# Longformer attention fused with a squared-ReLU expert layer: the order of work in batch 0, and where batch 2's waiting time is filled

## The chip, the cores and the metric

The kernel runs on one NeuronCore of a Trainium2 chip. The core has five engines with a queue of instructions each: TensorE (PE in the profile, its weight loads PEld), VectorE (DVE), ScalarE (ACT), GpSimd (POOL) and SyncE (SP). Sixteen DMA engines move data between the device memory (HBM) and the core's on-chip SBUF; transfers issued by POOL go through the queue q0 (software_dynamic), those of SP and ACT through q1 and q10 (hardware_dynamic). Matrix products land in PSUM, eight banks of 128 x 512 float32.

The metric is the device time of one execution in microseconds (us), as the median of several runs. A profiled execution is one more run with every instruction recorded; its span runs from the first to the last instruction of the program, and its own time is a little more than its span.

## What is computed

```python
B, H, S, D = 8, 8, 576, 64           # q, k, v: (B, H, S, D); 8 global tokens
scores = q @ k.T / sqrt(D)
mask = abs(i - j) <= 32  or  i is global  or  j is global
attn = softmax(where(mask, scores, -1e9))
x = (attn @ v).transpose(0, 2, 1, 3).reshape(4608, 512)
h = maximum(x @ w_in, 0)             # w_in: (512, 2048)
out = (h * h) @ w_out                # w_out: (2048, 512)
```

All inputs and the output are float32; the kernel computes in float16 with float32 sums.

## The kernel before

**Tiling.** The attention goes by pairs of heads: 8 batches of 4 pairs, numbered i = 4 b + hp. The 576 queries of a pair are padded to 608 columns (four groups of 144 tokens and the 8 global tokens again after each) and handled in two halves of 304. For a half, `sc_mm` makes the scores of the windows (S^T, keys on the partitions) in a PSUM tile `at`; `sc_exp` (ACT) takes their exponential; `sc_mask` (DVE) multiplies it with the 0/1 mask. In batch 0, where `added` says so, the mask is instead added to the scores by a product of the identity with the tile `far`. `pv_mm` multiplies with v and with ones into another `at` tile, `pv_rec` (ACT: logarithm, exponential) inverts the sums, `pv_mul` (DVE) writes the normalized result into `xT` (batch 0: first half into `xA`). `pv_sum` (DVE) collects the global queries' rows, and `scatter` (POOL, eight small copies at positions that are read from the input by `load_columns`) writes them over their tokens' columns.

**The expert layer** goes by chunks of 256 or 512 tokens, `CHUNKS`. For chunk 0, `mm1_half(u, half, tiles)` multiplies two of 16 blocks of w_in's columns with 256 tokens; `tiles` are the four groups of 128 input features, one for each pair of heads, so that the sum over pairs can stop after some of them and go on later. `mm2` adds up the output in four parts. From chunk 1 on, `mm1` (8 products) is followed by `mm2_fast`, which makes the second product from seven block products (Strassen's scheme, 14 pieces of 16 products): `g_sum` (DVE) adds blocks of the squared activations, and `weight_sum(p)` (DVE, once each for p = 1, 3, 4, 6, 7) adds blocks of w_out into the buffer `early`.

**Order.** Every engine runs its instructions in the order in which the program lists them. Batch 0's is written out by hand (lines 900 to 1013): the second query half of pair 0 and of pair 1 is mixed in among the first halves of pairs 2 and 3. From batch 1 on, expert work stands in a list `fills` of `(n, function, arguments)`, where n is the number of batches whose attention must be done. `fill(c)` adds c to a credit and takes entries off the list while the credit covers them and n <= `done[0]`; an `mm1` costs 0.65, an `mm2_fast` piece 1.54, an `mm1_half` or `mm2` 1. If the list's next entry isn't allowed yet, unused credit is dropped. `take(n)` takes n entries. In batch 1 a pair gets `fill(1)`, `fill(1)`, `fill(2)`; after it stands `fill(3)`; from batch 2 on each pair gets `fill(4)` between its scores and its `pv_mm` and `fill(4)` behind. `done[0]` is set to b only after the first `fill` of batch b.

**Buffers.** PSUM holds three `at` tiles (two banks each) and two `mm` tiles while batch 0 runs, then `open_psum(2, 4)` closes that pool and opens one with two and four; a tile of the new pool can be written once the last reader of the banks is done. The buffer `wide[0]` chooses whether a product is one instruction of 128 columns of weights or two of 64, which run side by side.

**Loads.** Batches 0 and 1 load tokens as they lie and transpose them on PE (`transpose`, `place_k`, `place_q`); later batches are written to a scratch in HBM and read through DMA transposes (`fetch_transposed`). POOL issues, in order: tokens of pairs 2 and 3, their values of v (L162, L166), the gather of the global rows of v (L442), the four parts of w_in (L979), the tokens of batch 1 (pair 4, then 5 to 7 together, L152), after the `scatter` of pairs 0 to 2 the first two parts of w_out (L1005), after that of pair 3 the other two (L1012), `scatter(0)`, the gathers, batch 2's loads. SP issues k and v of pairs 0 and 1, and then a small transfer called `gate` (L1015) that reads w_in's third part, and so holds back what SP issues behind it until that part has landed: v of batch 1, four pairs of 288 KB each (L162, L166). `values1` (DVE, L470) casts a pair of them to float16 before its `pv_mm`.

Of the kernel before, what the change touches and what calls it, by code (L numbers as in the profile page):

```python
# [8 lines left out]
FP32 = mybir.dt.float32  # L9
# [4 lines left out]
ALU = mybir.AluOpType  # L14
# [36 lines left out]
def kernel(  # L51
# [30 lines left out]
    def sbt(name, shape, dtype, bufs=1, tag=None):  # L82
        return sb.tile(shape, dtype, name=name, tag=(tag or name), bufs=bufs)

    psum = {}

    def open_psum(at, mm):
        if psum:
            psum["stack"].close()
        psum["stack"] = ExitStack()  # L90
        psum["pool"] = psum["stack"].enter_context(
            tc.tile_pool(name=f"ps{at}", bufs=1, space=bass.MemoryType.PSUM)
        )
        psum["bufs"] = {"at": at, "mm": mm}

    def pst(tag, shape, dtype=FP32):
        return psum["pool"].tile(shape, dtype, name=tag, tag=tag, bufs=psum["bufs"][tag])

    open_psum(3, 2)

    FW = TJ * D
    stf = sbt("stf", [P, 2, 4 * FW], FP32)
# [54 lines left out]
    def fetch_values(eng, b, hp, to=None):  # L157
        hs = slice(2 * hp, 2 * hp + 2)
        to = stv[:, :, hs] if to is None else to
        n = NT - 1  # L160
        for h in range(2):
            eng.dma_start(  # L162
                out=to[8 : 8 + KT, 0:n, h],
                in_=v[b, 2 * hp + h, 0 : KT * n].rearrange("(t s) d -> s t d", s=KT),
            )
        eng.dma_start(  # L166
            out=to[8 : 8 + KN[n], n],
            in_=v[b, hs, KT * n : S].rearrange("h s d -> s h d"),
        )
# [58 lines left out]
    ones = sbt("ones", [1, P], FP16)  # L228
    nc.vector.memset(ones, 1.0)
    nc.vector.memset(onesb, 1.0)  # L230
    nc.vector.memset(stv[0:NG, :, 0 : 2 * 2], 0.0)
    for vt in vts[2:NHP]:
        nc.vector.memset(vt[0:NG], 0.0)
    pidx = sbt("pidx", [P, 4], I32)
    nc.gpsimd.iota(pidx, pattern=[[0, 4]], base=0, channel_multiplier=1)
    icb = sbt("icb", [P, 4], I32)
# [49 lines left out]
    for kt in kts:  # L286
        nc.vector.memset(kt[:, 4, 8 + KN[4] : P], 0.0)

    for vt in vts[0:NHP]:
        nc.gpsimd.memset(vt[96:P, 4], 0.0)  # L290
    for i in range(2, NHP):
        fetch_tokens(nc.gpsimd, "k", i)
        fetch_tokens(nc.gpsimd, "q", i)
    for i in range(2, NHP):
        fetch_values(nc.gpsimd, 0, i, vts[i])


    wide = [False]
# [77 lines left out]

    far = sbt("far", [P, SCW0 + SCW[1]], FP16)

    def mask_globals(mg, half):
        for t, so, c0, w in (WIN0, WIN[1])[half]:  # L380
            for grp in range(4):
                lo, hi = max(grp * GRP, c0), min(grp * GRP + GTOK, c0 + w)
                lo, hi = max(lo, KT * t + 8 * grp), min(hi, KT * (t + 1) + 8 * grp)
                if lo < hi:
                    o = MB[half] + so + lo - c0
                    a = lo - half * BANKC
                    nc.scalar.activation(
                        out=mask[0:NG, o : o + hi - lo], in_=mg[0:NG, half, a : a + hi - lo],
                        func=AF.Identity, bias=1.0, scale=-1.0,
                    )  # L390

    def mask_added(half):
        r = slice(MB[half], MB[half] + (SCW0, SCW[1])[half])
# [330 lines left out]
    for part in range(4):  # L724
        for m in range(TC // P):
            fills.append((1, mm2, (0, m, part)))
    W1, W2 = 0.65, 1.54
    for c, (t0, T) in enumerate(CHUNKS[1:], 1):
        n = (t0 + T + S - 1) // S
        for x in range(NFF * T // TC):  # L730
# [14 lines left out]
    def fill(n):  # L745
        credit[0] += n
        while fills and fills[0][0] <= done[0]:
            cost = {mm1: W1, mm2_fast: W2}.get(fills[0][1], 1) * share[0]
            if credit[0] < cost / 2:
                break  # L750
            credit[0] -= cost
            take(1)
        else:
            credit[0] = min(credit[0], 0)

    share = [1.0]

    gsum = {}
    gxs = {}
# [75 lines left out]
    def pv_sum(i, half):  # L835
        b, hp = divmod(i, NHP)
        av = accs[(i, half)]
        if half == 0 or b:
            if hp == 0 and half == 0:
                gsum[b] = sbt("gs", [P, 2, NHP, 2, NG], FP32, bufs=2)  # L840
            nc.vector.tensor_reduce(
                out=gsum[b][:, half, hp],
                in_=av[:, :, :, GTOK:GRP].rearrange("p e k g -> p e g k"),
                axis=AX.X, op=ALU.add,
            )
        if (half == 0 and b == 0 and hp >= NHP - 2) or (half and b and hp == NHP - 1):
            gs = gsum[b][:, 0]
            a, z = (0, NHP) if b else (0, NHP - 1) if hp < NHP - 1 else (NHP - 1, NHP)
            if b:
                nc.vector.tensor_tensor(out=gs, in0=gs, in1=gsum[b][:, 1], op=ALU.add)  # L850
            gr = sbt("gr", [P, NHP, NG], FP32, bufs=2)
            if a == 0:
                gxs[b] = sbt("gx", [P, NHP, NG], FP16, bufs=2)
            nc.vector.reciprocal(out=gr[:, a:z], in_=gs[:, a:z, 1])
            nc.vector.tensor_tensor(
                out=gxs[b][:, a:z], in0=gs[:, a:z, 0], in1=gr[:, a:z], op=ALU.mult
            )
# [10 lines left out]
    def pv(i, half):  # L868
        pv_mm(i, half)
        pv_rec(i, half)  # L870
        pv_sum(i, half)
        pv_mul(i, half)
# [11 lines left out]
            nc.gpsimd.tensor_copy(out=xb[:, :, ds(gv[g], 1)], in_=gxs[b][:, pairs, g : g + 1])  # L884


    wv = moe_w_in.rearrange("(t p) f -> p t f", p=P)
    wo = moe_w_out.rearrange("(t p) m -> p t m", p=P)

    pool = nc.gpsimd  # L890

    def values1(i):
# [20 lines left out]
    transpose("q", 0)  # L913
    place_q(0, act)
    keep_warm(2)
    gather_index()
    gs0 = gather_rows(0, "v")
    casts0(1)
    cast_values(vec, 0)
    sc_mm(0, 0)  # L920
# [2 lines left out]
    values_sum(0)  # L923
    sc_exp(0, 0)
    place_k(1, act)
    place_q(1)
    values_place(0, act)
    mask_globals(mg, 1)
    cast_values(vec, 1)
    sc_mm(1, 0, 2)  # L930
    sc_exp(1, 0)
    transpose("k", 2, 3)
    transpose("q", 2)
    pv_mm(0, 0, 1)
    mask_added(1)
    place_k(2, act)
    pv_rec(0, 0)
    place_q(2)
    sc_mm(0, 1, 1)
    sc_exp(0, 1)  # L940
    pv_sum(0, 0)
    pv_mul(0, 0)
    values_sum(1)
    sc_mm(2, 0, 1)
    values_place(1, act)
    transpose("k", 3)
    transpose("q", 3)
    sc_exp(2, 0)
    place_k(3, act)
    place_q(3)  # L950
    pv_mm(1, 0)
    pv_mm(0, 1)
    values_sum(2)
    pv_rec(1, 0)
    values_place(2, act)
    pv_sum(1, 0)
    sc_mm(3, 0)
    values_sum(3)
    sc_exp(3, 0)
    values_place(3, vec)  # L960
    pv_mul(1, 0)
    pv_mm(2, 0)
    pv_rec(0, 1)
    pv_mul(0, 1)
    pv_rec(2, 0)
    pv_sum(2, 0)
    pv_mul(2, 0)
    sc_mm(1, 1)
    pv_mm(3, 0)
    sc_exp(1, 1)  # L970
    pv_rec(3, 0)
    pv_sum(3, 0)
    pv_mul(3, 0)
    pv_mm(1, 1)
    sc_mm(2, 1)
    sc_mm(3, 1)
    gather_store(0, gs0, "v")
    for i in range(4):
        pool.dma_start(out=w_in[:, :, ts(i, 512)], in_=wv[:, :, ts(i, 512)])  # L979
    def transposes1(i):  # L980
        transpose("k", i)
        transpose("q", i)
# [4 lines left out]
        fetch_tokens(pool, nm, NHP)  # L987
    for nm in "kq":
        fetch_tokens(pool, nm, NHP + 1, NHP - 1)
    load_columns()  # L990
    scatter(0, slice(0, NHP - 1), xA)
    pv_rec(1, 1)
    sc_exp(2, 1)
    sc_exp(3, 1)
    pv_mul(1, 1)
    sc_mask(2, 1)
    sc_mask(3, 1)
    open_psum(2, 4)
    wide[0] = True
    for u in range(0, 8, 2):  # L1000
        mm1_half(u, 0, range(NDM - 1))
    pv(2, 1)
    pv(3, 1)
    for j in range(2):
        pool.dma_start(out=w_out[:, ts(j, 4), :], in_=wo[:, ts(j, 4), :])  # L1005
    scatter(0, slice(NHP - 1, NHP), xA)
    nc.scalar.copy(out=xT[:, :, 256:HS], in_=xA[:, :, 256:HS])
    for u in range(0, 8, 2):
        fills.pop(0)
        mm1_half(u, 0, range(NDM - 1, NDM))  # L1010
    for j in range(2, 4):
        pool.dma_start(out=w_out[:, ts(j, 4), :], in_=wo[:, ts(j, 4), :])  # L1012
    scatter(0)
    gate = dram.tile([1, 8], FP16, name="gate")
    nc.sync.dma_start(out=gate, in_=w_in[0:1, 0, 2 * 512 : 2 * 512 + 8])  # L1015
# [6 lines left out]
    gs1 = gather_rows(1)  # L1022
    nc.gpsimd.memset(vbs[0][96:P, NT - 1], 0.0)
    gather_store(1, gs1)
    take(2)
    transposes1(NHP)
    take(2)
    done[0] = 1
    for vt in vts[NHP:]:
        nc.vector.memset(vt[96:P, 4], 0.0)  # L1030
# [26 lines left out]
    scatter(1)  # L1057
    fetch_transposed(2 * NHP)
    fetch_transposed(2 * NHP + 1)
    fill(3)  # L1060
    wide[0] = False

    for i in range(2 * NHP, B * NHP):
        b, hp = divmod(i, NHP)
        if i in (2 * NHP + 1, 4 * NHP + 1):
            c = b // 2 + 1
            if c < 4:
                gather_store(c, gather_rows(c))
        scores(i, 0)
        scores(i, 1)  # L1070
        if i + 2 < B * NHP:
            fetch_transposed(i + 2)
        if b == 2:
            for p in ((3, 4), (6, 7), (1,), ())[hp]:
                weight_sum(p)
            if hp == 0:
                nc.gpsimd.memset(vbs[1][96:P, NT - 1], 0.0)
        fill(4)
        if hp == 0:
            done[0] = b  # L1080
            share[0] = 2 / 3 if b == 4 else 1
        pv_mm(i, 0)
        pv_mm(i, 1)
        for half in range(2):
            pv_rec(i, half)
            pv_sum(i, half)
            pv_mul(i, half)
        if hp == NHP - 1:
            scatter(b)
        fill(4)  # L1090
        if b + 1 < B and hp < 3:
            if hp == 0:
                open_batch(b + 1)
                fetch_batch_globals(b + 1)
            if hp < 2:
                fetch_batch(b + 1, "kq"[hp])
            else:
                fetch_batch_values(b + 1)
    take(len(fills))
    psum["stack"].close()  # L1100


# [28 lines left out]
```

## Time and profile before

| | |
|---|---|
| Median of 14 runs | 328.25 us (327.02 to 330.98) |
| Profiled execution, its own time | 327.72 us |
| Its span | 326.0 us |
| PE busy | 308.1 us (94%) |
| DVE busy | 244.7 us (75%) |
| ACT busy | 200.9 us (62%) |
| POOL busy | 127.1 us (39%) |
| Mean granted TensorE clock | 0.994 |

A line of the profile's table of stretches gives the stretch, its length, and for PE, PEld, DVE, ACT and POOL the busy time and the number of instructions; then the granted TensorE clock (1.00 is full), the mean busy share of the DMA engines, and what they moved in GB/s. A line of the timeline gives start, length, engine, source line, operation, what it writes and reads, its shape and how many were merged; brackets tell how long the engine was idle before and what ended it.

### The profile page before, as it was taken

To read this page: it belongs to the slowest core of one execution; us is meant where nothing else is said; L and a number is where in the kernel's file an instruction comes from. 1 tells how busy PE (TensorE), PEld (TensorE's weight loads), DVE (VectorE), ACT (ScalarE), POOL (GpSimd) and SP (SyncE) were. 2 spreads that over 40 slices of the span, in tenths; PEclk is the share of its full clock that TensorE was granted. 3 is DMA by queue.
4 is the path that set the end of the run, shared out by engine and by line. 5 is a ranking of instruction groups with operands and counts; after the bars stand their busy time and mean duration, and the time that the engine had idled before them with its cause. 6 is when DMAs were issued, how large, how long until landed. Compare 5 with 4: busy or idle time off the path is not lost.

```text
span 326.0 us, 11606 instructions
## 1 busy us (share of the span) xinstructions
PE 308.1 (94%) x4827; PEld 234.1 (72%) x4827; DVE 244.7 (75%) x595; ACT 200.9 (62%) x378; POOL 127.1 (39%) x222
## 2 busy tenths in 40 slices
PE   5887899999989999999999999999999999999995
PEld 3665767445578758975899856985698569868994
DVE  7864588657997788677867869876987698667465
ACT  2575678636856685768457387658765876373150
POOL 8946578258702950289000962049302000100000
PEclk9997999999999999999999999999999999999999
DMA  8999999999993999399924599659985301200211
GB/s 191 146 201 200 195 191 155 147 112 211 137 102 93 153 172 112 74 149 190 128 76 103 51 182 143 76 131 163 147 91 127 95 4 34 99 2 2 95 37 66
DMA packets 149492, 38.98 MB, mean 120 GB/s; under 512 B 132696, under 2 KB 148872, under 8 KB 149440
## 3 DMA queue, kind: packets, MB, share of 16 engines
q0 software_dynamic: 97872, 17.08, 67.4%
q1 hardware_dynamic: 51150, 20.57, 32.9%
q8 instruction: 38, 0.62, 0.8%
q10 hardware_dynamic: 418, 0.59, 0.7%
q14 instruction: 14, 0.11, 0.1%
HBM read 37.80 MB, written 17.29 MB: 169 GB/s over the span
## 4 chain that ended last, share of the span: by engine, by line
PE 38%; issue 27%; POOL 9%; DMA 7%; DVE 6%; ACT 3%; POOLq 1%; DVEq 0%; ACTq 0%
PE mm L305 34%; DMA qscr<-in_q_dram 4%; DMA kscr<-in_k_dram 3%; POOL xT L884 3%; POOL kscr L183 2%; PE at L822 2%; DVE gt L556 2%; DVE mix L641 2%; PE at L781 2%; POOL stf L212 2%; ACT er L790 1%; POOL gstk L442 1%; DVE xT L863 1%; POOL gstq L442 1%; POOL gstv L442 1%
## 5 line engine op out<-in xcount | busy, mean ns | idle before, releaser
L305 PE MATMUL mm<-xT,w_in 128*64 128x512 f16 (+2 forms) x1216 | 122.5, 351 | 0.2 <-POOL xT L884 0.2
L305 PEld LDWEIGHTS <-w_in 128*64 128x64 f16 (+1 forms) x1280 | 79.9, 109 | 45.6 <-issue 3.4
L554 ACT ACTIVATE rl<-mm 128x512 f16<-128x512 f32 x128 | 74.3, 600 | 36.7 <-PE mm L305 32.7
L556 DVE TENSOR_TENSOR gt<-rl 128x512 f16<-128x512 f16 x128 | 52.8, 421 | 24.4 <-ACT rl L554 20.8
L884 POOL COPY xT<-gx 128x4 f16 x64 | 17.8, 278 | 135.0 <-DVE xT L863 131.6
L305 PEld LDWEIGHTS <-mix 128*64 128x64 f16 x1280 | 68.8, 110 | 1.6
L790 ACT ACTIVATE er<-at 128x880 f16<-128x880 f32 x58 | 49.7, 904 | 15.4 <-PE at L781 13.9
L641 DVE TENSOR_TENSOR mix<-gt 128x1024 f16<-128x1024 f16 (+1 forms) x82 | 52.8, 670 | 0.2
L800 DVE TENSOR_TENSOR et<-er,mask 128x880 f16<-128x880 f16 x58 | 35.7, 616 | 18.5 <-ACT er L790 18.0
L305 PE MATMUL mm<-early,mix 128*64 128x256 f16 x768 | 45.4, 273 | 0.0
L832 ACT ACTIVATE rec<-at 128x288 f32<-128x288 f32 x64 | 25.8, 403 | 27.8 <-PE at L822 22.9
L305 PEld LDWEIGHTS <-gt 128*64 128x64 f16 (+1 forms) x596 | 33.1, 109 | 11.3 <-DVE gt L556 3.6
L305 PE MATMUL mm<-early,gt 128*64 128x256 f16 x512 | 32.2, 274 | 2.5 <-DVE gt L556 2.4
L863 DVE TENSOR_TENSOR xT<-at,rec 128x288 f16<-128x288 f32 x60 | 27.1, 452 | 9.5 <-ACT rec L833 9.0
L305 PE MATMUL mm<-w_out,mix 128*64 128x256 f16 x512 | 30.9, 273 | 0.0
L822 PE MATMUL at<-et,onesb 128*64 128x192 f16 (+5 forms) x400 | 29.8, 225 | 0.0
L833 ACT ACTIVATE rec<-rec 128x288 f32<-128x288 f32 x64 | 28.4, 443 | 2.0
L676 DVE TENSOR_TENSOR ot<-mm,pt 128x512 f32<-128x512 f32 (+1 forms) x36 | 22.7, 631 | 6.5 <-ACT pt L701 5.2
L183 POOL DMA_DIRECT2D kscr<-in_k_dram x30 | 26.3, 1064 | 2.2 <-DMA w_out<-in_moe_w_out_dram 1.8
L190 POOL DMA_DIRECT2D qscr<-in_q_dram x24 | 23.9, 1392 | 0.0
L701 ACT COPY pt<-mm 128x512 f32<-128x512 f32 (+1 forms) x18 | 9.7, 540 | 20.5 <-PE mm L305 20.5
L822 PEld LDWEIGHTS <-onesb 128*64 128x64 f16 x400 | 21.9, 110 | 0.7
(125 smaller groups left out, 315.4 us busy)
## 6 DMA issues: line engine op xcount, KB each, us to landing
out_dram<-ot SPq DMA_DIRECT2D x32, 256.0 KB
qscr<-in_q_dram POOLq DMA_DIRECT2D x24, 144.0 KB
kscr<-in_k_dram POOLq DMA_DIRECT2D x24, 120.0 KB
w_in<-in_moe_w_in_dram POOLq DMA_DIRECT2D x4, 512.0 KB
w_out<-in_moe_w_out_dram POOLq DMA_DIRECT2D x4, 512.0 KB
early<-in_v_dram SPq DMA_DIRECT2D x12, 120.0 KB
stf<-in_v_dram POOLq DMA_DIRECT2D x12, 120.0 KB
s16b<-in_v_dram POOLq DMA_DIRECT2D x12, 120.0 KB
```

The costliest lines, as they stand in the source:

```text
L183: nc.gpsimd.dma_start(out=kscr[b][r0 : r0 + KN[t]].rearrange("s (h d) -> s h d", d=D), in_=k[b, :, KT * t : KT * t + KN[t]].rearrange("h s ...
L305: nc.tensor.matmul(to[r], weights[:, r], moving, **flags)
L554: nc.scalar.activation(out=rl, in_=ph, func=AF.Relu)
L556: nc.vector.tensor_tensor(out=gt[:, :, 0:T], in0=rl, in1=rl, op=ALU.mult)
L641: nc.vector.tensor_tensor(out=gsums[p][:, lo:hi, 0:TH], in0=g[0], in1=g[1], op=op)
L790: nc.scalar.activation(out=er[:, :, 0:W], in_=scs.pop((i, half))[:, :, 0:W], func=AF.Exp, bias=0.0, scale=scale)
L800: nc.vector.tensor_tensor(out=et[:, :, 0:W], in0=er[:, :, 0:W], in1=mask[:, MB[half] : MB[half] + W].unsqueeze(1).to_broadcast((P, 2, W)), ...
L822: nc.tensor.matmul(acc[D * e : D * e + D, x, o : o + w], onesb if x else vt[:, t, e], et[:, e, so : so + w], start=(n == 0), stop=(n == le ...
L832: nc.scalar.activation(out=rec, in_=av[:, 1, :, 0:GTOK], func=AF.Ln)
L833: nc.scalar.activation(out=rec, in_=rec, func=AF.Exp, scale=-1.0)
L863: nc.vector.tensor_tensor(out=(xT if x0 else xA)[:, hp, x0 : x0 + HS].rearrange("p (k x) -> p k x", k=2), in0=av[:, 0, :, 0:GTOK], in1=rec ...
L884: nc.gpsimd.tensor_copy(out=xb[:, :, ds(gv[g], 1)], in_=gxs[b][:, pairs, g : g + 1])
```

## The change

Batch 0 runs the first halves of all four pairs, then half of the first expert products (the two input groups of pairs 0 and 1), then the scores of the second halves of pairs 0 and 1, the other half of those products, and the rest of the second halves with more expert products between. `gx` is finished two pairs at a time, and `scatter` runs for pairs 0 and 1, then for 2 and 3. w_in's first part is issued between the values of pairs 2 and 3, its second behind the gather, its third and fourth behind the first `scatter`; batch 1's tokens come behind the second `scatter`, and w_out's four parts together behind them. The third `at` tile lies in a PSUM pool of its own, which alone is closed to make room for two more `mm` tiles. Zeros that DVE and POOL wrote at the start are copied by ACT; `place_q(1)` moves from DVE to ACT; the second half's global mask is made by DVE from an SBUF copy `mgs`. Behind batch 1 stand five times `fill(2.6)` with a `weight_sum` behind each, in place of `fill(3)` and of the weight sums in batch 2, and batch 2's remaining entries are divided evenly over its eight fills. Line numbers of new lines are not those of the profile.

```diff
-    psum = {}
-    def open_psum(at, mm):
...
-    open_psum(3, 2)
+    banks_of = {"at": 0, "mm": 0}
+    pools = {}
+    def open_psum(name, tags):
...
+    psum_base = open_psum("base", {"at": 2, "mm": 2})
+    psum_more = open_psum("third", {"at_more": 1})
     def pst(tag, shape, dtype=FP32):
-        return psum["pool"].tile(shape, dtype, name=tag, tag=tag, bufs=psum["bufs"][tag])
+        n = banks_of[tag]
+        banks_of[tag] += 1
+        more = tag + "_more"
+        if more in pools and (n % 3 == 0 if tag == "at" else n % 2):
+            tag = more
+        pool, bufs = pools[tag]
+        return pool.tile(shape, dtype, name=tag, tag=tag, bufs=bufs)
...
-    nc.vector.memset(stv[0:NG, :, 0 : 2 * 2], 0.0)
+    zeros = idle[0:NG].unsqueeze(1)[:, :, 0 : 4 * D].to_broadcast((NG, NT, 4 * D))
+    nc.scalar.copy(out=stv[0:NG, :, 0:4].rearrange("p t h d -> p t (h d)"), in_=zeros)
     for vt in vts[2:NHP]:
-        nc.vector.memset(vt[0:NG], 0.0)
+        nc.scalar.copy(out=vt[0:NG].rearrange("p t e d -> p t (e d)"), in_=zeros[:, :, 0 : 2 * D])
+        nc.scalar.copy(out=vt[96:P, 4].rearrange("p e d -> p (e d)"), in_=idle[96:P, 0 : 2 * D])
+    for vt in vts[0:2]:
+        nc.vector.memset(vt[96:P, 4], 0.0)
...
-    for vt in vts[0:NHP]:
-        nc.gpsimd.memset(vt[96:P, 4], 0.0)
...
-    for i in range(2, NHP):
-        fetch_values(nc.gpsimd, 0, i, vts[i])
+    fetch_values(nc.gpsimd, 0, 2, vts[2])
+    fetch_w_in(0)
+    fetch_values(nc.gpsimd, 0, 3, vts[3])
...
-    W1, W2 = 0.65, 1.54
+    COST = {mm1: 0.65, mm2_fast: 1.54}
...
+    def left():
+        return sum(COST.get(fn, 1) for n, fn, _ in fills if n <= done[0])
...
-            a, z = (0, NHP) if b else (0, NHP - 1) if hp < NHP - 1 else (NHP - 1, NHP)
+            a, z = (0, NHP) if b else (hp - 1, hp + 1)
...
-    place_q(1)
+    place_q(1, act)
+    gather_index()
+    gs0 = gather_rows(0, "v")
+    gather_store(0, gs0, "v")
+    fetch_w_in(1)
+    load_columns()
     values_place(0, act)
-    mask_globals(mg, 1)
+    act(out=mgs, in_=mg[0:NG, 1, 0:BANKC])
...
-    sc_mm(0, 1, 1)
-    sc_exp(0, 1)
...
-    pv_mm(0, 1)
...
+    pv_mul(1, 0)
+    scatter(0, slice(0, 2), xA)
+    fetch_w_in(2)
+    fetch_w_in(3)
+    sc_mm(3, 0, 1)
...
+    mask_globals(mg, 1)
+    mask_added(1)
+    pv_mm(3, 0, 1)
...
-    sc_mm(2, 1)
-    sc_mm(3, 1)
-    gather_store(0, gs0, "v")
-    for i in range(4):
-        pool.dma_start(out=w_in[:, :, ts(i, 512)], in_=wv[:, :, ts(i, 512)])
+    scatter(0, slice(2, NHP), xA)
...
     for nm in "kq":
         fetch_tokens(pool, nm, NHP)
     for nm in "kq":
         fetch_tokens(pool, nm, NHP + 1, NHP - 1)
-    load_columns()
-    scatter(0, slice(0, NHP - 1), xA)
...
-    open_psum(2, 4)
+    pools.pop("at_more")
+    psum_more.close()
+    psum_more = open_psum("fourth", {"mm_more": 2})
     wide[0] = True
     for u in range(0, 8, 2):
-        mm1_half(u, 0, range(NDM - 1))
-    pv(2, 1)
-    pv(3, 1)
-    for j in range(2):
-        pool.dma_start(out=w_out[:, ts(j, 4), :], in_=wo[:, ts(j, 4), :])
-    scatter(0, slice(NHP - 1, NHP), xA)
-    nc.scalar.copy(out=xT[:, :, 256:HS], in_=xA[:, :, 256:HS])
+        mm1_half(u, 0, range(2))
+    scores(0, 1)
+    scores(1, 1)
     for u in range(0, 8, 2):
         fills.pop(0)
-        mm1_half(u, 0, range(NDM - 1, NDM))
-    for j in range(2, 4):
-        pool.dma_start(out=w_out[:, ts(j, 4), :], in_=wo[:, ts(j, 4), :])
+        mm1_half(u, 0, range(2, NDM))
+    pv(0, 1)
+    pv(1, 1)
+    nc.scalar.copy(out=xT[:, :, 256:HS], in_=xA[:, :, 256:HS])
+    take(1)
+    scores(2, 1)
+    transposes1(NHP)
+    scores(3, 1)
+    take(1)
+    pv(2, 1)
+    take(1)
+    pv(3, 1)
+    for j in range(4):
+        fetch_w_out(j)
     scatter(0)
...
-    take(2)
-    transposes1(NHP)
-    take(2)
     done[0] = 1
...
-    fill(3)
+    done[0] = 2
+    for p in (3, 4, 6, 7, 1):
+        fill(2.6)
+        weight_sum(p)
     wide[0] = False
+    slot = left() / 8
...
-        if b == 2:
-            for p in ((3, 4), (6, 7), (1,), ())[hp]:
-                weight_sum(p)
-            if hp == 0:
-                nc.gpsimd.memset(vbs[1][96:P, NT - 1], 0.0)
-        fill(4)
+        if i == 2 * NHP:
+            nc.gpsimd.memset(vbs[1][96:P, NT - 1], 0.0)
+        fill(slot if b == 2 else 4)
         if hp == 0:
             done[0] = b
...
-        fill(4)
+        fill(slot if b == 2 else 4)
```

`fetch_w_in(i)` and `fetch_w_out(j)` issue one part of w_in or w_out from POOL.

## The prediction

> **What bounds the kernel now.** I read the table of stretches first.
>
> ```profile
> 20.00:30.00 10.00, 6.64 (x135) 4.80 (x130) 6.87 (x21) 7.75 (x16) 3.53 (x12) 0.93 1.26 207
> 50.00:60.00 10.00, 10.00 (x179) 6.79 (x174) 8.62 (x26) 7.37 (x16) 8.14 (x10) 1.00 2.12 153
> 90.00:100.00 10.00, 9.03 (x176) 8.03 (x174) 10.00 (x22) 5.75 (x11) 0.00 (x0) 1.00 0.96 82
> 25.15:28.57 3.42, 1.64 (x42) 1.22 (x38) 2.25 (x9) 3.36 (x7) 2.18 (x9) 1.00 1.27 203
> 28.57:31.98 3.41, 2.85 (x14) 2.02 (x15) 0.94 (x2) 0.46 (x1) 2.86 (x11) 0.50 1.31 196
> ```
>
> From 40 us on PE is full: its idle is 0.97 us in 90 to 100 (where DVE is at 10.00 of 10) and a few tenths elsewhere, so what the change can win lies ahead of 40 and at 92. In 20 to 30 PE idles 3.4 of 10, and after 25.15 to 28.57 (PE busy 1.64 of 3.42) the granted clock is 0.50 for 3.4 us. The DMA engines meanwhile move about 200 GB/s without a pause.
>
> The timelines of PE, POOL, SP and DVE tell what is late.
>
> ```profile
> 29.13 4.15 PE L305 MATMUL mm<-mix,w_in 128*128 128x256 f16 x24 [1.48 <-ACT er L790]
> 92.67 2.05 PE L305 MATMUL mm<-early,gt 128*64 128x256 f16 x34 [0.97 <-DVE gt L556]
> 13.95 3.08 POOL L979 DMA_DIRECT2D w_in<-in_moe_w_in_dram  x4
> 25.81 2.02 POOL L884 COPY mix<-gx 128x3 f16 x8 [6.03 <-DVE mix L863]
> 25.51 0.24 SPq L1015 DMA_DIRECT2D gate<-w_in  x1
> 48.01 0.55 DVE L470 CAST early<-early 128x512 f16<-128x512 f32 x2
> 50.73 0.46 DVE L863 TENSOR_TENSOR xT<-at,rec 128x288 f16<-128x288 f32 x1 [0.23 <-ACT rec L833]
> 51.84 0.26 PE L822 MATMUL at<-et,early 128*64 128x160 f16 x2
> ```
>
> The first expert products start at 29.13. Line 5 is the gate: SP starts batch 1's v 0.7 us after it. The last three lines are pair 5: cast of its v, the `pv_mul` that frees the `at` tile, its `pv_mm`. The DMA queues over 29.8 to 45.3 us (packets, MB, share):
>
> ```profile
> q0 software_dynamic: 2595, 2.34, 92.2%
> q1 hardware_dynamic: 2415, 0.62, 31.3%
> ```
>
> While POOL's queue is full, v of batch 1 gets 0.62 MB in 15.5 us, 40 GB/s. Pairs 4 and 5 are 2 x 288 KB = 0.59 MB, so pair 5's v has come at 45.3, 2.7 us ahead of its cast: the only small margin in batch 1.
>
> **Part by part.** *Start.* DVE loses memsets of 1.12 and 0.67 us and gains two of 0.11: 1.6 earlier. ACT's copies (some 2.5 us by the sizes of DVE's) lie in its 4.3 us wait for q until 6.41. POOL's four memsets go, 0.70, so its loads start 0.7 earlier. First scores at about 8.4 in place of 9.89; bounds 0 and 1.6.
>
> *First halves.* Out of the middle go, on PE, two scores and one `pv_mm` of second halves (0.76, 0.7, 0.44 from start to start), on ACT two exponentials and a `pv_rec` (0.91, 0.90, 0.85). In come `place_q(1)` on ACT (0.83), the copy `mgs` (0.4, by the four mask pieces' 0.55) and, on DVE just ahead of pair 3's `pv_sum`, mask pieces and `far` (0.5 + 0.48); warm-up products stay near 0.11 each. Following PE from start to start (scores 0.9 with `far`, a transpose 0.45, `pv_mm` 0.51, values' sum 0.3), pair 3's `pv_mm` falls to 21.4, before 24.88; `pv_mul(1, 0)` ends at 20.6, POOL's first scatter runs 20.7 to 22.7 (2.02 as before), the second 24.4 to 26.4. `load_columns` now lies ahead of it on POOL and is hidden: in before it ended inside the 6.03 of idling.
>
> *Products.* First at 22.7, not 29.13, at full clock: 24 take 24 x 1.05/8 = 3.15 instead of 4.15. Then, in order: 16 products 2.1, two scores 0.7 each, 16 products (behind the second scatter) to 28.6, two `pv_mm` 0.9, then entries, scores and transposes, each waiting a little for ACT. Batch 1's first scores stand at 36.0 against 41.16, with three entries taken and not four (1.05 each): a lead of 4.1 us, if the data is there.
>
> *Is it?* The third part of w_in is now issued behind the first scatter, at 22.7. POOL's queue has run dry: parts one and two, issued at 9.8 and 14, are through at about 19. In before it took 2 us from the issue at 13.95 to full flow. So part three flows from 24.5 and, with 0.52 MB at 200 GB/s, is through at 27.1; in before the gate opened 1.2 behind the last byte (1.56 MB moved from 16 to 24.3, gate 25.51). It now opens at 28.3, 2.8 later. POOL's queue holds 4.3 MB from then on (half of w_in, tokens 1.18, w_out 2.1), full until about 50, so v still gets 40 GB/s, and pair 5's comes at 48.1 plus 0.8 to 1.2 to land. Behind its cast on DVE stand two squares, the mask product, another square, `pv_sum` and `pv_mul(4, 1)`: 3.2 us in before (48.01 to 51.19), 2.7 without the waits. `pv_mm(5, 0)` then falls to 51.6: the lead is gone, and one entry less is done. PE idles some 3 us there, and 2 us near 39, where the first second-half product waits for `scatter(0)` (POOL, behind `pv_mul(3, 1)`; it took 3.2) and pair 4's v. Term: 1.05 - 0.25 = **+0.8**; bounds: -4.1 (v not late) and +2.5 (scatter copies at 0.41 each, as at 36 to 39 us, twice). I take the middle, since pair 5's margin of 2.7 equals the gate's delay. Tokens of pairs 5 to 7 come at 37.4 and are used at 37.4: no term.
>
> *Behind batch 1.* 13 credits buy nine `mm2` (0.92 each) and six `mm1` (0.89): 13.6 us of PE. Weight sums (2.35 for two) take DVE 5.9, its copies and squares 5.0: 10.9 of 13.6, hidden; without that cover the stall at 92 comes back earlier. Batch 2's transposes, issued from 60.8 in before, have over 10 us more time. DVE is spared 5.9 in batch 2: of 0.97 and 0.2 stalled there I take **-0.9**; bounds -1.2 and 0.
>
> *Batch 3's first slot.* Chunk 1 holds 16 x 0.65 + 14 x 1.54 = 32 credits. Four are spent ahead, 28 go evenly over batch 2: none is left. The first `fill` of batch 3 stands ahead of `done[0] = 3`, chunk 2 isn't allowed, so `scores` and `pv_mm` of pair 12 stand side by side. In before 32 products fill that place. The chain of waits shows its price at another pair:
>
> ```profile
> 98.11 0.51 PE at L781 x12
> 98.63 1.71 ACT er L790 x2
> 100.37 0.63 DVE et L800
> 101.04 0.57 PE at L822 x12
> ```
>
> From the scores' start at 98.04 to the second half's `pv_mm` end at 101.6 are 3.56 us, in which PE works 0.5 + 0.8: **+2.2**, bounds 1.6 (only the first half waited for) and 2.5.
>
> *The clock.* The row at 25.15 to 28.57 shows PE half busy and the clock halved after; it cost 4.15 - 3.15 = 1.0. Three stalls of 2 to 3 us are of that kind: 0 to 3.0; they are nearest to that one row's single drop: **+1.0**. The Trainium skill, in "TensorE: Matmul & The Clock Gate", section "HAM oscillation — how this bites in real kernels", warns of idle gaps above about 3.4 us only; the row's largest gap was 1.48, so row and rule differ. By the rule this term is 0 and the time 330.3.
>
> *At nothing:* 128 columns in one instruction or two of 64 (`mm2` 2.76/3 against 3.64/4), PSUM's new pools (still three `at`, later two and four `mm`, in the same rotation), w_out's later issue (first used by the products at 54.5, and there by 42).
>
> Sum: 0.8 - 0.9 + 2.2 + 1.0 = +3.1 on the profiled execution's 327.7 (326.0 and 1.7 around), 330.8. The median of the runs is 0.5 above that execution: **331.3**.
>
> **Rivals.** *The lead survives.* v isn't late, because the first scatter ends before 20 or the hardware queue gets more than 40 GB/s. -4.1 - 0.9 + 2.2 = -2.8: 325.5. For it: PE's 3.4 us of idling in 20 to 30 is real. Against: q1's share over 15 us, and w_in's place behind the scatter.
> *Half of it survives.* The gate opens 1.3 later, not 2.8; the lead left pays for batch 3's slot and one drop of the clock or none: 328.3.
> *It doesn't do what it says.* POOL's copies take 0.41 each and the products start after 25: gate another 1.5 to 2 later, pair 5 and 6 both wait, two or three drops: 334. For it: 3.17 for eight copies at 36 us. Against: 2.02 at 25.8, with DVE nearly as busy.
>
> **How the numbers follow.** The forecast 0.46, the third rival 0.12, half a lead 0.17, the whole lead 0.25. Within 0.3% (1 us) can't be told from no change. So faster 0.25, same 0.17, slower 0.58. The range: from the whole lead's 325.5, half of whose chance lies above 325.8, to 334; outside lie about 0.13 below and 0.06 above. The forecast's own range is 329.5 to 333: 0 to 2 drops of the clock, and 1 us of the gate.
>
> **What would show it.** The first products at 22.7 and batch 1's first scores near 36 show the early steps right. The gate near 28.3, the cast of pair 5 idle until a DMA at about 49, and `pv_mm(5, 0)` at 51 to 52 show the middle; a `pv_mm(5, 0)` below 49.5 refutes it, and the lead survives. PE's idling of some 2 us ahead of `pv_mm` of pair 12, DVE not ending a stall in batch 2, and a granted clock of 0.5 after a stall show the rest. Wrong it is if SP's v flows earlier than 31 us, or if pair 12's `pv_mm` starts behind other products.

## The result and the profile after

The changed kernel took 332.1 us (median of 10 runs, 330.5 to 333.9), the kernel before beside it 328.2 (47 runs): a ratio of 1.0108, 95% interval 1.008 to 1.0136, slower by 2.6 to 4.5 us. Ratios are taken over the fast executions of both kernels (those more than 1.5% above their kernel's fastest are left out), so they differ a little from the ratio of the medians. The forecast was 331.3. The profiled execution of the changed kernel took 333.3 us, its span 331.6 (before 326.0), with a mean granted clock of 0.978.

Where the 5.6 us of span went is read from the table of stretches of the changed kernel first (length, busy us of PE, PEld, DVE, ACT, POOL, granted clock, DMA share, GB/s):

```profile
20.00:22.00 2.00, 1.96 (x42) 1.33 (x39) 1.90 (x7) 1.40 (x4) 0.50 (x3) 1.00 0.10 19
22.00:24.00 2.00, 1.28 (x26) 1.23 (x27) 1.49 (x9) 1.47 (x4) 1.55 (x7) 1.00 0.00 0
24.00:26.00 2.00, 2.00 (x21) 1.37 (x20) 0.79 (x3) 0.00 (x0) 1.76 (x7) 1.00 0.41 31
...
30.38:33.79 3.41, 1.37 (x34) 0.88 (x32) 2.37 (x5) 2.32 (x6) 2.48 (x4) 1.00 1.28 198
33.79:37.20 3.41, 1.88 (x33) 1.49 (x34) 1.21 (x4) 0.64 (x2) 0.00 (x0) 0.50 1.27 179
37.20:40.62 3.42, 3.42 (x25) 2.23 (x24) 1.25 (x3) 1.96 (x4) 0.00 (x0) 0.50 1.25 194
44.03:47.44 3.41, 1.49 (x20) 1.07 (x21) 2.29 (x6) 0.65 (x2) 2.65 (x6) 1.00 1.22 198
47.44:50.86 3.42, 3.42 (x26) 2.46 (x21) 2.08 (x6) 2.11 (x5) 2.93 (x4) 0.50 1.18 188
108.88:112.30 3.42, 1.51 (x28) 1.10 (x24) 3.21 (x9) 2.02 (x3) 1.28 (x5) 1.00 0.46 125
112.30:115.71 3.41, 3.27 (x34) 2.49 (x35) 1.81 (x6) 1.59 (x4) 3.06 (x7) 0.50 0.85 160
...
90.00:100.00 10.00, 10.00 (x172) 7.98 (x170) 8.90 (x22) 7.21 (x15) 4.22 (x5) 1.00 2.17 149
```

Two things are new. From 20 to 26 us the DMA engines stand nearly idle (19, 0 and 31 GB/s), where in the kernel before they moved about 200. In MB: 0.08 in these 6 us, against 1.21 in the kernel before. And there are three places with a half-busy PE (1.37, 1.49 and 1.51 of 3.4 us), each followed by a clock of 0.50: 13.7 us in all, against 3.4 before (28.57 to 31.98). The last row shows that the 0.97 us of idling in 90 to 100 is gone.

The timelines of the changed kernel name what PE waited for; the lines are those shown of before, and the new waits:

```profile
23.39 0.60 PE L327 MATMUL mm_more<-mix,w_in 128*128 128x256 f16 x4 [0.65 <-POOL mix L917]
35.32 0.69 PE L532 MATMUL mm_more<-identity,s16b 96*64 96x96 f16 x12 [2.59 <-DMA s16b<-in_q_dram]
45.95 1.03 PE L327 MATMUL mm_more<-xT,w_in 128*128 128x256 f16 x8 [2.17 <-POOL xT L917]
55.10 0.26 PE L855 MATMUL at<-et,early 128*64 128x160 f16 x2
112.44 0.35 PE L855 MATMUL at<-et,s16b 128*64 128x160 f16 x2 [1.48 <-DVE et L833]
...
21.38 1.96 POOL L917 COPY mix<-gx 128x2 f16 x8 [5.96 <-DVE mix L896]
23.49 1.49 POOL L307 DMA_DIRECT2D w_in<-in_moe_w_in_dram  x2
28.79 0.24 SPq L1041 DMA_DIRECT2D gate<-w_in  x1
49.99 0.46 DVE L896 TENSOR_TENSOR xT<-at,rec 128x288 f16<-128x288 f32 x1 [0.28 <-ACT rec L866]
50.37 1.06 DVE L500 CAST early<-early 128x512 f16<-128x512 f32 x2
```

Batch 1's first scores stand at 41.45; in the kernel before they are this line:

```profile
41.16 0.37 PE L781 MATMUL at<-qt,kt 64*128 64x160 f16 x6
```

The first products start at 23.39 (before 29.13), so the new order of batch 0 works. But w_in's last two parts are issued only at 23.49, behind the first scatter, and the queue has been dry until then. The tokens of pair 4 come behind them and PE waits 2.59 us for q; the clock halves, `pv_mul(3, 1)` and with it `scatter(0)` slip, PE waits 2.17 more, and pair 5's `pv_mm` starts at 55.10 (before 51.84). In this execution pair 5's v was not late: its cast has no idle time ahead of it. At 112.44 stands pair 12's `pv_mm`, behind the empty slot.

### The profile page after: what moved, and what is told of

Read it like the earlier page. It is cut to its first block, busy times and chain, and to the rows that moved or that the text cites. A ratio compares the mean times of both kernels' runs of the same rounds, so it can differ in the third digit from the quotient of the medians.

```text
span 331.6 us, 11505 instructions
## 1 busy us (share of the span) xinstructions
PE 312.9 (94%) x4783; PEld 235.9 (71%) x4783; DVE 244.8 (74%) x596; ACT 205.1 (62%) x382; POOL 131.1 (40%) x218
## 4 chain that ended last, share of the span: by engine, by line
issue 39%; PE 33%; POOL 19%; DMA 3%; POOLq 2%; DVE 2%; ACT 0%; DVEq 0%
PE mm_more L327 15%; PE mm L327 14%; POOL xT L917 4%; POOL kscr L191 3%; DMA qscr<-in_q_dram 3%; PE at L855 3%; POOL stf L220 2%; POOL qscr L198 2%; POOL s16b L220 1%; PE at L814 1%; POOLq L912 1%; POOL mix L917 1%; POOL s16b L160 1%; POOL mix L160 1%; POOLq L917 1%
## 5 line engine op out<-in xcount | busy, mean ns | idle before, releaser
L917 POOL COPY xT<-gx 128x4 f16 x64 | 20.3, 317 | 140.4 <-DVE xT L896 136.8
L327 PE MATMUL mm_more<-xT,w_in 128*64 128x512 f16 (+3 forms) x596 | 72.3, 356 | 2.4 <-POOL xT L917 2.4
L327 PE MATMUL mm<-xT,w_in 128*64 128x512 f16 (+3 forms) x596 | 71.6, 353 | 0.0
L584 ACT ACTIVATE rl<-mm_more 128x512 f16<-128x512 f32 x64 | 38.2, 597 | 28.8 <-PE mm_more L327 28.1
L584 ACT ACTIVATE rl<-mm 128x512 f16<-128x512 f32 x64 | 38.4, 600 | 13.2 <-PE mm L327 11.3
L327 PE MATMUL mm_more<-early,mix 128*64 128x256 f16 x512 | 31.1, 273 | 0.0
L814 PEld LDWEIGHTS <-kt 64*128 64x128 f16 x400 | 12.3, 95 | 13.8 <-issue 12.7
L814 PE MATMUL at<-qt,kt 64*128 64x192 f16 (+5 forms) x390 | 19.9, 226 | 2.2 <-DVE xT L896 2.2
```

The lines of the kernel that those rows point to most:

```text
L327: nc.tensor.matmul(to[r], weights[:, r], moving, **flags)
L584: nc.scalar.activation(out=rl, in_=ph, func=AF.Relu)
L814: nc.tensor.matmul(sc[:, e, so : so + w], kt[r, t, :], qt[r, c0 : c0 + w], start=not added(i, half), stop=True, skip_group_check=True,)
```

## The experiments

Ratios are against the kernel before, run beside them: its medians were 325.85, 325.69 and 325.87 us in the three sets e1 to e4, e5 to e8 and e9 to e12, so that these sets can be laid side by side. The first pair of profiles comes from a set at 328.2.

| | ratio (95%) | profiled time, us | pair 5's `pv_mm`, us |
|---|---|---|---|
| changed kernel again (e12) | 1.0132 (1.0087 to 1.0177) | 329.2 | 52.34 |
| e1, w_in early | 1.0027 (0.9987 to 1.0068) | 324.3 | 47.86 |
| e2, w_in and tokens early | 1.0103 (1.0053 to 1.0152) | 330.3 | 53.90 |
| e3, nine slots | 1.0053 (1.0017 to 1.0089) | 332.0 | 54.98 |
| e4, before with the second part | 1.0096 (1.0059 to 1.0133) | 328.1 | 51.14 |
| e5, e4 with nine slots | 1.0008 (0.9976 to 1.0040) | 324.7 | 50.41 |
| e6, e1 and e3 | 0.9954 (0.9926 to 0.9981) | 323.0 | 48.21 |
| e7, e6 with tokens of pair 4 earlier | 0.9954 (0.9926 to 0.9982) | 326.8 | 52.01 |
| e8, products on zeros | 1.0120 (1.0095 to 1.0146) | 328.6 | 51.72 |
| e9, gate earlier | 1.0173 (1.0136 to 1.0210) | 330.4 | 53.92 |
| e10, another order of loads | 0.9990 (0.9960 to 1.0021) | 327.7 | 52.96 |
| e11, second part taken back | 1.0154 (1.0109 to 1.0199) | 328.6 | 51.76 |

**e1: all of w_in ahead of the first scatter.**

```diff
-    fetch_w_in(1)
+    for i in range(1, NHP):
+        fetch_w_in(i)
...
-    fetch_w_in(2)
-    fetch_w_in(3)
     sc_mm(3, 0, 1)
```

> The third and fourth part of w_in go out behind the second, ahead of the first scatter; the tokens of batch 1 stay behind the second scatter. As predicted (v of pair 5, held back by the gate, sets batch 1): the gate opens 4 to 5 us earlier, near 24; pv_mm(5, 0), at 55.1 in the changed kernel, falls by 3 us or more, and the time to 328 to 329. Rival from the changed kernel's trace (the tokens of pair 4 set it, which the gate does not hold): POOL's queue is dry again while it copies, q of pair 4 lands at 34 to 36 as now (35.3), batch 1's first scores stay at 40 to 42, and the time stays at 331 to 332.5. Third (only batch 3's first slot and the clock cost): 331.5 to 332.5 with batch 1 earlier and no gain.

Measured: 326.7 us, 0.8% (against the first ratio) to 1.05% (against e12's) below the changed kernel. Two stretches of e1, and PE's first scores of batch 1 and `pv_mm` of pair 5:

```profile
20.00:30.00 10.00, 8.43 (x121) 6.22 (x116) 4.86 (x19) 6.70 (x14) 7.34 (x23) 1.00 1.09 179
100.00:110.00 10.00, 7.94 (x122) 5.92 (x120) 7.72 (x21) 6.75 (x14) 5.88 (x13) 1.00 0.87 121
...
36.09 0.37 PE L814 MATMUL at<-qt,kt 64*128 64x160 f16 x6 [0.48 <-DVE xT L896]
47.86 0.26 PE L855 MATMUL at<-et,early 128*64 128x160 f16 x2
```

The DMA engines move 179 GB/s in 20 to 30, where the changed kernel had 92. The gate opens at 24.42, batch 1's first scores stand at 36.09 (changed kernel 41.45 and, in e12, 38.65), pair 5's `pv_mm` at 47.86. So the lead is there if w_in isn't behind the scatter; the place of two DMA issues in POOL's program decided it. The rival on the tokens falls: they are still issued behind the second scatter (25.77), and PE doesn't wait for those of pair 4. The second stretch shows that batch 3's empty slot is untouched: 2.06 us of PE's idling.

**e2: w_in and the tokens of batch 1 ahead of the first scatter.**

```diff
-    fetch_w_in(1)
+    for i in range(1, NHP):
+        fetch_w_in(i)
+    for nm in "kq":
+        fetch_tokens(pool, nm, NHP)
+    for nm in "kq":
+        fetch_tokens(pool, nm, NHP + 1, NHP - 1)
     load_columns()
```

> w_in's third and fourth part and all tokens of batch 1 go out ahead of the first scatter, so that POOL's queue never runs dry. If the late loads are what took the lead: the wait for q of pair 4 (2.59 us at 35.3) goes, batch 1's first scores fall from 41.5 to 36 to 38, at least one of the two early drops of the clock (34 and 47 us) goes, and the time is 327 to 328.5. If it is the scatter of batch 0 on POOL (2.17 us at 45.95) that decides: the scores move, but the first product of the second half stays near 45 to 46, and the time is 330.5 to 332. If the tail alone makes the loss: 331.5 to 332.5.

Measured: 330.1 us, a miss: e1's gain is gone. POOL's timeline in e2:

```profile
19.51 0.81 POOL L160 DMA_DIRECT2D s16b<-in_q_dram  x1
24.10 3.86 POOL L917 COPY mix<-gx 128x2 f16 x16 [3.78 <-DVE mix L896]
```

The first scatter starts at 24.10 (e1 20.64), 3.78 us after the last issue, although the last `pv_mul` that it needs ended at 20.30. Between the two on POOL stand only the value loads of `load_columns`; in e1, too, 3.57 us lie between the last issue and the copies. So they seem to take POOL about 3.6 us that the profile doesn't count as busy. This is inferred from these gaps (3.58 us in e6), not measured alone; that the gap is the same behind three issues and behind seven speaks for the loads and against the issues, and in e12 and e9, where the loads are done in time, the scatter starts 0.08 us behind its `pv_mul`. Four more issues (2.8 us) ahead of them made the scatter late; PE waited 4.4 us for it, and the clock fell to half.

**e3: nine slots in place of eight on the changed kernel; e4 and e5: the second part alone on the kernel before, with eight and with nine.**

```diff
-    slot = left() / 8
+    slot = left() / 9
```

> Chunk 1's entries are shared out over nine slots, so that batch 3's first slot holds some. Theory (the empty slot costs 2.2, and the drop of the clock behind it 1.7 by its 3.41 us at half): PE's waits of 0.57 and 1.48 us ahead of pair 12's second scores and pv_mm go, the clock stays at 1.00 at 112, and the time falls by 2 to 4 us, to 328 to 330. Rival (the products put there are missing elsewhere in batch 2, where PE then waits): 0 to 1 us less, with waits of PE in 83 to 110 of 1 us or more.

> The kernel before with the change's second part alone: weight sums and fills behind batch 1, batch 2's entries in eight equal slots. By the prediction's terms: -0.9 for the stall at 92 and +2.2 for batch 3's first slot, +1.3 in all without a drop of the clock and about +3 with one at half for 3.4 us: 329.5 to 331.2. Rival (the loss lies in batches 0 and 1 alone): 327 to 328, below before by the 0.9.

> The kernel before with the change's second part, but batch 2's entries shared over nine slots, so that pair 12 has some. Theory (e4's loss of about 1% is the empty slot, 2.06 us of PE's idling ahead of pair 12, and the clock after it in some runs): ratio to before 0.994 to 1.002, 2.5 to 4 us under e4. Rival (weight sums and fills behind batch 1 cost something of their own): ratio 1.004 or more.

Measured: e3 328.1 us, about 0.55 to 0.8% below the changed kernel (its profiled execution, 332.0, lies 3.9 above its median, so its total gives no size here). e4 329.3, 3.1 us above before by the ratio; e5 325.7, 0.9% below e4. The expectation of e4 came to about +3 with a drop of the clock behind the slot, but e4's profile shows none there: from pair 8's first scores to pair 16's it takes 57.33 us and e5 54.74, at a clock of 1.00 in both. There the slot costs 2.59 us by itself. The empty slot thus costs 0.5 to 0.9% in each pairing of the two, and the rest of the second part costs nothing that can be measured. Nor does it bring anything that can be: 0.9 us would be a ratio of 0.997, just outside e5's interval. The kept traces do show a smaller wait: from pair 5's `pv_mm` to pair 16's scores PE idles 1.57 of 84.44 us in before and 0.51 of 83.44 in e5. Why the runs don't show that microsecond stays open.

**e6: e1 and e3 together.**

> e1 and e3 together: w_in's third and fourth part ahead of the first scatter, and nine slots. Theory (both losses are apart and add up: e1 took 0.8% off the changed kernel, e3 0.55%): ratio to before 0.994 to 0.999, PE without the 2.06 us ahead of pair 12. Rival (they share one cause, the clock): ratio 1.001 to 1.004, as e1.

Measured: 323.5 us against 325.7, ratio 0.9954 (0.9926 to 0.9981): faster than both kernels, and the two repairs add up. PE's first-half scores of pair 8 and of pair 16 stand so in e6:

```profile
76.02 0.56 PE L814 MATMUL at<-qt,kt 64*128 64x160 f16 x12
...
132.64 0.36 PE L814 MATMUL at<-qt,kt 64*128 64x160 f16 x6
```

and in e12, which is the changed kernel itself:

```profile
80.59 0.56 PE L814 MATMUL at<-qt,kt 64*128 64x160 f16 x12
...
138.89 0.36 PE L814 MATMUL at<-qt,kt 64*128 64x160 f16 x6
```

Between the two marks PE runs 897 matmul instructions in either kernel, in 56.62 and in 58.30 us. The slot costs 1.68 us where the clock stays up. The other traces agree: with nine slots e3, e7 and e10 take 56.62 to 56.63, with eight e1, e2 and e9 58.29 to 58.31. In the first profile of the changed kernel, with the drop at 112.3, the same stretch took 59.52 (82.92 to 142.44): 2.9.

**e7 and e10: tokens of pair 4 between the scatters** (e10 also puts w_in's fourth part behind the second scatter).

```diff
     scatter(0, slice(0, 2), xA)
+    for nm in "kq":
+        fetch_tokens(pool, nm, NHP)
```

> e6, and the tokens of pair 4 go out between the two scatters in place of behind both. If what is left of the loss is the wait for q of pair 4 (0.81 us in e1 at 38.8): that wait goes and the ratio is 0.2 to 0.4% below e6. If POOL's queue is what counts (two issues of 0.65 us each put the second scatter later): the first product after the second scatter waits 1.2 us more and the ratio is the same as e6's or above.

> e6 with another order on POOL: w_in's third part behind the second, tokens of pair 4 between the scatters, w_in's fourth part behind the second scatter. Theory (e6 still waits 2.4 us in all for tokens of pair 4 and 0.8 to 1 for scatter(0)): the waits for tokens go, the second scatter is not later than in e6 (23.95), and the ratio is 0.990 to 0.994. Rival (what is gained at 30 to 40 us is waited for behind it, as in e7): 0.995 to 0.998.

Measured: 324.1 and 325.4 us, no better than e6. The expectation of e7 read a line wrongly: the 0.81 us in e1 at 38.8 were for q of pairs 5 to 7. In e7 no wait for tokens is left and the one for `scatter(0)` is 1.90; in e10 PE waits 1.76 us for q of pairs 5 to 7. Their profiled executions lie 2.7 and 2.3 us above their medians, with PE's products on `far` of nearly twice the usual length at 13 us already (1.28 in place of 0.68 us), so their early marks aren't set beside e6's.

**e8: products on zeros in PE's three long waits.** They write tiles that are overwritten.

```diff
-        transpose("q", i)
+        transpose("q", i, 12 if i == NHP else 0)
...
+        if half and u == 0:
+            warm(ph.rearrange("p j x -> p (j x)"), 10)
...
-        pv_mm(i, 0)
+        pv_mm(i, 0, 9 if i == 3 * NHP else 0)
```

> The changed kernel with products on zeros in its three long waits of PE (12 ahead of the transpose of q of pair 4, 10 ahead of the first product of the second half, 9 ahead of pair 12's pv_mm; 0.2 us each), so that the waits stay but PE is not idle in them. Theory (three drops of the clock, 13.6 us at half, cost 3 us or more of the loss): the granted clock stays at 1.00 or drops once, and the time falls by 2 to 4 us to a ratio of 0.998 to 1.005. Rival (the drops fall where PE waits for others anyway): the clock stays up and the time is within 1 us of the changed kernel's ratio of 1.011.

Measured: the clock stays at 1.00, and the time is 328.9 us, ratio 1.0120, against 1.0132 for the changed kernel. So the rival holds within what can be measured: the drops were not the bulk of the loss. The six runs took 328.6 to 330.5 us at a mean clock of 0.998 and more; the kernel before, in its runs with such a clock beside them, took 324.3 to 325.3. The products on zeros aren't free (pair 8 to pair 16 takes 58.63 us here and 58.30 in e12), so e8 doesn't give the price of the drops. PE's timeline of e8 shows why:

```profile
31.82 2.76 PE L327 MATMUL mm_more<-idle 128*128 128x512 f16 x12
40.63 2.33 PE L327 MATMUL mm_more<-idle 128*128 128x512 f16 x10
51.72 0.26 PE L857 MATMUL at<-et,early 128*64 128x160 f16 x2 [1.26 <-DVE xT L898]
```

With PE at full clock pair 5's `pv_mm` starts at 51.72, and now waits: DVE stood idle for 1.54 and 0.89 us ahead of the two parts of the cast, until that pair's v had landed. In e12 DVE waits as long for the same v, but PE, at half clock for part of the time, shows no wait there: a wait that the half clock had covered comes out in e8.

**e9: the gate reads w_in's second part**, which opens it 7 us earlier (21.34), so that v comes into the idle DMA time.

```diff
-    nc.sync.dma_start(out=gate, in_=w_in[0:1, 0, 2 * 512 : 2 * 512 + 8])
+    nc.sync.dma_start(out=gate, in_=w_in[0:1, 0, 512 : 512 + 8])
```

> The changed kernel with the gate reading w_in's second part in place of the third, so that SP sends v of batch 1 some 5 us earlier, into the time in which POOL's queue is dry; tokens and w_in stay where they are. Theory (as predicted: v of pair 5 sets batch 1, as in e3 and e8 where DVE waited 3.04 and 1.54 us for it): no such wait of DVE, pv_mm(5, 0) before 50, ratio 1.002 to 1.007. Rival (the tokens of pair 4 set it, as in the changed kernel's own profile): 1.009 to 1.013.

Measured: 331.2 us, ratio 1.0173, above the range of the theory and that of the rival, and no gain on the 1.0132 of the changed kernel (the intervals overlap, so that it is slower is not shown). PE's and DVE's timelines of e9:

```profile
30.01 1.05 PE L327 MATMUL mm_more<-mix,w_in 128*128 128x256 f16 x8 [0.95 <-DMA w_in<-in_moe_w_in_dram]
34.65 0.69 PE L532 MATMUL mm<-identity,s16b 96*64 96x96 f16 x12 [3.30 <-DMA s16b<-in_k_dram]
...
50.03 1.07 DVE L500 CAST early<-early 128x512 f16<-128x512 f32 x2
```

The cast of pair 5's v no longer waits, but w_in and k of pair 4 do come late: v took their bytes. From 26 to 35 us q0, which carries w_in and the tokens, moved 1.39 MB and q1 0.34; in e12 it was 1.61 and 0.15. What is short is not v or the tokens alone but what the DMA engines can move from 26 us on, after the dry stretch. The order counts too: e9 had moved 0.4 MB more than e12 from 20 to 26 us, but of v, which is needed later than the tokens.

**e11: the second part taken back on the changed kernel.**

```diff
-    done[0] = 2
-    for p in (3, 4, 6, 7, 1):
-        fill(2.6)
-        weight_sum(p)
+    fill(3)
```

(with the weight sums and `fill(4)` of batch 2 as before).

> The changed kernel with the second part taken back: fill(3) behind batch 1, weight sums in batch 2, four credits a slot. What is left is the new order of batch 0 with its loads. By the prediction's terms (+0.8 for the lead, up to +1.0 for the clock): ratio 1.002 to 1.006. Rivals: the start costs nothing (e4's 0.96% alone makes the loss): 0.998 to 1.001; or it makes nearly all of it: 1.008 or more.

Measured: 330.2 us, ratio 1.0154, by its number the last of the three. But it isn't a clean separation, since entries that lag by one slot are now spread over later batches: from pair 16's to pair 28's scores it takes 112.6 us, where the changed kernel takes 110.1 (e12). It refutes that the new start costs nothing. It also has the weight sums in batch 2 with DVE 9.70 of 10 busy there, and yet PE busy for 10.00 of 90 to 100.

**e12: the changed kernel once more.**

> The changed kernel once more, for a second profile and for a ratio beside the three others. If its first profile is a usual one, PE waits over 2 us for q of pair 4 again and the clock drops at 34 and 47 us; if that was one execution's bad luck, as e3 and e8 suggest, the wait for q of pair 4 is under 1 us and DVE waits for v of pair 5 near 50. Ratio 1.008 to 1.014 in both cases.

Measured: 330.1 us, ratio 1.0132. DVE's timeline of e12:

```profile
48.75 0.43 DVE L500 CAST early<-early 128x512 f16<-128x512 f32 x1 [1.52 <-DMA early<-in_v_dram]
50.06 0.70 DVE L500 CAST early<-early 104x128 f16<-104x128 f32 x1 [0.88 <-DMA early<-in_v_dram]
```

In this execution PE waited 0.80 and 0.90 us for tokens of pair 4 and not 2.59, and DVE did wait for pair 5's v, which was there at about 50.0. So either load can be the last one, from one execution to the next. The clock still fell, once between 32 and 38.8 us and once between 42.2 and 49.1.

**The account.** e5 has the start of the kernel before, no drop of the clock in its profile and no empty slot, and a ratio of 1.0008; so it serves as the base:

```profile
50.41 0.26 PE L822 MATMUL at<-et,early 128*64 128x160 f16 x2
```

A kernel with the new start should differ from it by (pair 5's `pv_mm` minus 50.41, plus 1.05 for the entry less that is done by then, 8 products), plus 1.68 if it has eight slots:

| | start | slot | sum | profiled time less e5's 324.7 |
|---|---|---|---|---|
| e12 | +3.0 | 1.7 | +4.7 | +4.5 |
| e8 | +2.4 | 1.7 | +4.0 | +3.9 |
| e9 | +4.6 | 1.7 | +6.2 | +5.6 |
| e2 | +4.5 | 1.7 | +6.2 | +5.6 |
| e1 | -1.5 | 1.7 | +0.2 | -0.5 |
| e6 | -1.2 | 0 | -1.2 | -1.8 |
| e7 | +2.6 | 0 | +2.6 | +2.0 |
| e10 | +3.6 | 0 | +3.6 | +3.0 |

The two terms account for these eight to within 0.7 us, always from above; most of that rest lies behind pair 16's scores, from which e6 and e12 take 188.6 us to the end and e5 189.2. Three profiles don't fit by these terms alone. The first one of the changed kernel has +7.4 for a measured +8.6: the drop of the clock behind its slot is the other 1.2. e3 has +5.6 for +7.3: its pair 6 is another 2.3 late. e11 has +2.4 for +3.9: its later batches take longer, as said.

## Why the prediction was right, and where it was not

The time (331.3 against 332.1), the sign and the place of both losses were right. By its own steps:

- *Start.* First scores at 8.65 (8.4 predicted), first products at 23.39 (22.7), gate at 28.79 (28.3): right to 0.7 us. SP issues batch 1's v at 29.54, and its queue moves the first bytes between 32 and 33 us, not before the 31 that would have shown the prediction wrong.
- *"The lead is gone", through w_in's place behind the scatter, the gate and pair 5's v.* The place is shown by e1, e6 and e12: with w_in early, batch 1's first scores stand at 36.09, as the 36.0 that was worked out if the data is there. v of pair 5 was predicted at 48.9 to 49.3 and its `pv_mm` at 51.6; e12 has 50.0 and 52.34, e8 51.72. The step's term, +0.8, was made against a profile of before that has a drop of its own: against that (51.84) it was 0.9 in e8 and 1.6 in e12. Against e5, without a drop, it is 2.4 and 3.0. In the first profile it was 4.3 against before, and there v of pair 5 didn't decide. The 3 us of PE's idling that the step saw ahead of pair 5 came in neither profile of the changed kernel; it is 1.26 in e8 and 3.36 in e3.
- *What the step left out.* "Tokens of pairs 5 to 7 come at 37.4 ... no term" looked at the wrong ones: the dry queue put back every transfer behind it, and pair 4's tokens come first. PE waited for them in both profiles of the changed kernel, 3.3 us in all in the first, which with two drops put batch 1's first scores at 41.45 in place of 36.0. And the gate is no cause by itself: e9 opened it early and gained nothing.
- *The stall near 39 for `scatter(0)`*: 2 us predicted, 2.17 and 2.22 measured, later (45.95, 43.19) as all of batch 1 is.
- *Batch 3's first slot*: +2.2 (1.6 to 2.5) predicted; 1.68 in the traces at full clock, 2.9 with a drop behind it, 2.59 on the kernel before (e4 against e5), 0.5 to 0.9% by the ratios.
- *The stall at 92*: -0.9 predicted. The wait is gone from the traces, but the runs don't show the credit: e5, which has only this left, gains nothing measurable (1.0008), and e11 lost the wait with the weight sums still in batch 2. That the weight sums caused it was argued, not shown.
- *The clock*: +1.0, one drop net. The first profile has two more than before, e12 one more. What they cost is not settled: e8 kept the clock up and came out 0.1% below e12, inside both intervals. Among 17 runs of the kernel before (with e9 to e12) the time goes with the clock: 324.3 to 324.8 us at 0.998 and more, 325.4 to 326.2 at 0.992 to 0.995, 327.3 to 327.8 at 0.988 to 0.990, some 1.3 to 1.6 us a step; what makes PE idle and what the lower clock adds can't be told apart there.

That 331.3 came so near to 332.1 is in part luck, because the errors run against each other: too little for the start (against a base without drops), a credit of 0.9 that the runs don't show, and 1.0 for the clock whose price stays open.

## What to carry to other kernels

When DMA issues are moved behind compute on the same engine, look at when the queue runs dry and count the bytes that are not moved then: every later transfer is put back, whichever wait shows it first, and letting one of them go earlier can make another late (e9). When entries of work are spread over slots, count the slots up to the point from which new work is allowed. POOL's time in loads of register values isn't in the busy rows here (some 3.6 us, inferred); look for it in the gap between its neighbours.

## What the runs showed of the hardware that was not expected

- A software queue that had run dry took about 2 us to flow again: issue at 23.49, 0 GB/s in 22 to 24, 31 GB/s in 24 to 26, 206 GB/s in 26 to 30. Without an issue from 15.41 to 23.49 the engines moved 0.08 MB in 20 to 26 us, where e1 moved 1.08.
- The clock fell to 0.50 after 3.4 us windows in which PE was still busy for 1.37, 1.49 and 1.51 us, with single waits of 2.59, 2.17 and 1.48 us at most. The Trainium skill ("TensorE: Matmul & The Clock Gate", section "HAM oscillation — how this bites in real kernels") warns of gaps above about 3.4 us; in these runs less was enough.
- The same waits of 0.57 and 1.48 us ahead of pair 12 brought a drop in the first profile of the changed kernel and none in those of e1, e4 and e12. Which executions drop thus changes from one to the next, and so do their times. No run here shows what decides it.
- Value loads of eight positions into registers seem to take POOL about 3.6 us (gaps of 3.57, 3.58 and 3.78 us in e1, e6 and e2), in which it shows as idle.
